# Agent attention with a maxout layer: one engine for each output tile of the last group, and new orders of work in the last batch

## The chip, the cores and the metric

The kernel runs on one core of a Trainium2 chip. The metric is the device time of one execution in microseconds; the runs shown of the kernel before have a median of 450.71 us (450.23 to 452.75, six runs). The profile comes from one execution, and its times count from the start of that execution's span.

## The reference

Four batches of 12544 queries, keys and values with 128 channels, and 49 agents per batch. First the agents attend to the keys and gather the values; then each query attends to the 49 agents; then a layer with three weight matrices takes the largest of three products and multiplies it with an output matrix:

```python
a2k = sm(agents, k)            # softmax(agents k^T / sqrt(128)), 49 x 12544 per batch
agent_v = a2k @ v              # 49 x 128 per batch
x = sm(q, agents) @ agent_v    # 12544 x 128 per batch
h = max(max(x @ w1, x @ w2), x @ w3)   # 50176 x 768
out = h @ w_out                # 50176 x 128
```

## The kernel before

Since x is a product with the small matrix agent_v, the kernel multiplies the weights with agent_v once per batch (the tile G, 49 rows at two heights, with columns for w2-w1, w3-w1 and the linear part through w1) and never forms x. It takes max(w1,w2,w3) as w1 plus the larger of (w2-w1) and the positive part of (w3-w1); the part w1 goes through the output matrix as a linear term.

The queries come in 49 groups (0 to 48) of 1024; 12 groups belong to a batch, and group 48 holds two row tiles of 128 of each of the four batches, so it has four parts (`parts_of`, L610). `q_group` (L617) names the steps of a group. For engine PE they are:

- scores `s` (L661) into a small PSUM tile, read by the exponentials `ex` on ACT (L669), and row sums `sum` (L673), read by the reciprocal `rec` on DVE (L680);
- for each of six column blocks f: `u`f (L694) and `v`f (L705), two matmuls each (eight in group 48). `a`f on ACT makes the positive part of u; `x`f on DVE takes the larger of v and a (L713) into the tile r. For f = 4 both `a4` and `x4` are on ACT, in place and then by L711;
- for each of the two output tiles o: `lin`o (L715, L718) starts the sum with two matmuls, and `oc`of (L722, L727) adds block f with four. `sc`o on DVE (L730, L734) scales it by the reciprocals into o_sb, and `st` (L739) stores a group with one DMA from SP.

In the text "38.x3" is step x3 of group 38. PSUM is short: all u and v tiles share three slots (`uv_tile`, L239), and scores, sums and output tiles share two (`small_tile`, L242). A step that opens a tile waits until the former holder of its slot has been read. The a tiles have three buffers, each r tile two, o_sb ten.

Keys and values of the next batch are worked through beside the queries (`k_group`, L509): group s of the queries carries a step of nine row tiles of keys, with `kc`, `vc`, `ea` on POOL (casts and the addition L547 to Eacc), `ks` and `kv` on PE, `ke` on ACT, `ka` on DVE. At a batch's end `k_tail` (L565) forms the new G: `red` (DVE, L574, over Eacc), `tot` (PE), `nrm` (DVE), products `p21` and `p31` (PE, L506), and their copies `e21` (DVE) and `e31a`, `e31b` (ACT). For the last batch this falls into groups 34 and 35.

The order is written by hand, as numbers: each step is filed under 6.0 times its group plus its place in a table, the list is sorted and emitted, and each engine runs its own instructions in that order. `places` (L808) chooses the table: KEY for most groups, LATE for groups 36 to 48, BORDER about a batch's end, OWN for single groups (34, 35, 36, 37, 47 and 48 among them), BATCH3 for the last `k_tail`. Stores are held back by up to seven groups (L824). Loads of q, their casts on POOL (`qc`) and, from group 36 on, transposes by DMA from SP (`turn_by_dma`, L657) run about two groups ahead.

Group 48 ends otherwise. Each of its two output tiles is scaled in halves, one per part, into four tiles o_end: half 2o by `end_scale` on DVE (L747, L749), half 2o+1 by `end_scale_scalar` on ACT (L752, L755, two instructions of 128 columns). Four stores of 128 KB (`end_store`, L757, L760) go from SP for parts 0 and 2 and from ACT for parts 1 and 3.

Of the kernel before, what the change touches and what calls it, by code (L numbers as in the profile page):

```python
# [25 lines left out]
    "oc14": 12.887, "oc12": 12.963, "oc13": 12.963, "sc1": 12.964, "st": 14.464,  # L26
}
LATE = {
    "s": -3.04749, "ex": -2.9048, "u1": -0.81512, "a1": -0.11576, "u2": 2.37421, "a2": 2.45765,
    "v1": 3.37564, "u3": 3.7004, "x1": 3.89334, "v2": 4.55864, "u0": 4.63, "a3": 4.65519, "x2": 4.7366,  # L30
    "a0": 5.00849, "v0": 5.38379, "u4": 5.77286, "x0": 6.25719, "a4": 6.54196, "u5": 7.04507,
    "v3": 7.1227, "x3": 7.44794, "v4": 7.51529, "lin1": 7.79655, "oc10": 8.14238, "sum": 8.14596,
    "rec": 8.17689, "oc12": 8.20379, "a5": 8.30536, "x4": 8.30648, "v5": 8.33752, "x5": 9.15285,
    "oc11": 9.49257, "oc13": 9.51825, "oc14": 10.09493, "lin0": 10.79959, "oc05": 10.84292,
    "oc15": 10.98413, "sc1": 11.49114, "oc02": 11.78965, "oc04": 11.82151, "oc00": 11.92155,
    "oc01": 12.02239, "oc03": 12.08397, "sc0": 12.87981, "st": 20.85007,
}

HEAD = {
# [27 lines left out]
        "st": 19.70003,  # L67
    },
    34: {
        "qt": -3.25348, "qe": -1.60938, "s": -1.08319, "ex": -0.07959, "ks": 0.24487, "ke": 0.69785,  # L70
        "u0": 0.71333, "a0": 1.42845, "v0": 1.46674, "u2": 1.55402, "ea": 1.95293, "u3": 2.01249,
        "sum": 2.04733, "kv": 2.10268, "a2": 2.26187, "a3": 2.44259, "u1": 3.00016, "x0": 3.08612,
        "v3": 3.16826, "rec": 3.3107, "ka": 3.48647, "a1": 4.24948, "x3": 4.28591, "v2": 4.7809,
        "u4": 4.96093, "x2": 5.54815, "a4": 6.34821, "u5": 6.35018, "a5": 6.53733, "v1": 6.53854,
        "v4": 6.56719, "x1": 6.7338, "x4": 6.84009, "v5": 6.91391, "x5": 6.9451, "lin1": 7.77018,
        "oc10": 8.3659, "lin0": 9.00035, "oc15": 9.04244, "oc04": 9.84141, "oc03": 10.06875,
        "oc01": 10.63146, "oc11": 10.91162, "oc00": 11.48787, "oc02": 11.69743, "oc05": 11.81297,
        "oc13": 11.92399, "sc0": 13.04207, "oc14": 13.24301, "oc12": 13.83351, "sc1": 15.27025,
        "st": 24.04256,
    },  # L80
    35: {
        "qt": -3.42697, "qe": -1.92735, "s": -1.33281, "ex": -1.31359, "ks": -0.92787, "sum": -0.87491,
        "ke": -0.36902, "kv": 0.32675, "ka": 0.59937, "rec": 0.88212, "u0": 0.88898, "a0": 0.90891,
        "v0": 1.17271, "u2": 1.45782, "a2": 2.00605, "u3": 2.51453, "x0": 2.59991, "v2": 2.93949,
        "a3": 3.20012, "u1": 3.23502, "a1": 3.44584, "x2": 3.51835, "v3": 3.942, "x3": 4.00627,
        "u5": 4.00643, "a5": 4.27302, "v5": 5.21895, "u4": 5.42122, "x5": 5.50884, "v1": 6.24909,
        "a4": 7.18659, "lin0": 7.89365, "oc03": 8.01405, "v4": 8.43263, "x1": 8.57785, "x4": 9.00519,
        "oc01": 9.40322, "oc02": 9.47513, "oc04": 10.01557, "oc00": 10.50745, "oc05": 10.70916,
        "lin1": 10.90156, "sc0": 11.20709, "oc15": 11.40347, "oc14": 11.51719, "oc11": 11.60961,
        "oc13": 13.16199, "oc12": 13.4014, "oc10": 13.57708, "sc1": 14.10054, "st": 28.07888,  # L90
    },
    36: {
        "s": -3.85762, "ex": -3.02118, "u1": -1.08192, "a1": 0.13487, "u2": 1.12084, "a2": 1.36634,
        "v2": 2.58017, "u0": 2.89822, "a0": 3.64302, "x2": 3.64864, "v1": 3.74492, "u3": 4.3491,
        "a3": 4.61245, "x1": 4.81452, "v0": 5.22302, "u4": 5.36733, "x0": 5.40904, "sum": 5.69395,
        "rec": 5.70943, "a4": 6.01497, "v3": 6.05388, "u5": 6.27145, "x3": 6.33451, "v4": 7.23655,
        "a5": 7.57697, "v5": 7.74872, "x4": 7.83644, "lin1": 7.8482, "oc10": 7.92453, "x5": 8.25933,
        "oc12": 8.53805, "oc14": 9.4705, "lin0": 10.11318, "oc00": 10.32008, "oc05": 11.08993,
        "oc11": 11.69579, "oc15": 11.95855, "oc13": 12.2097, "oc02": 12.27498, "sc1": 12.67367,
        "oc01": 13.63741, "oc04": 13.76201, "oc03": 14.31012, "sc0": 14.45082, "st": 20.04155,  # L100
    },
    37: {
        "s": -2.3763, "ex": -1.99168, "u1": -0.89023, "a1": -0.83864, "u2": 1.83631, "a2": 2.10039,
        "v2": 2.62074, "v1": 3.10251, "u0": 3.16911, "x2": 4.82079, "a0": 4.82575, "v0": 5.46426,
        "x1": 5.54152, "u3": 5.79276, "x0": 5.85326, "u5": 6.28625, "a3": 6.54158, "v3": 6.87889,
        "x3": 7.02476, "a5": 7.06215, "u4": 7.13124, "sum": 7.13155, "rec": 7.40011, "a4": 7.42192,
        "v5": 8.40138, "lin1": 8.44301, "x5": 8.50546, "oc11": 8.7139, "oc13": 8.85734, "v4": 9.11956,
        "oc10": 9.83416, "oc15": 9.91897, "lin0": 10.00468, "oc12": 10.1672, "x4": 10.46283,
        "oc02": 10.75773, "oc14": 10.97159, "oc01": 10.99548, "sc1": 11.08374, "oc05": 12.19635,
        "oc04": 12.41887, "oc00": 12.48727, "oc03": 12.57446, "sc0": 13.3308, "st": 13.63859,  # L110
    },
    47: {
        "s": -2.96572, "ex": -2.44054, "u1": -0.98286, "a1": -0.38292, "u0": 2.50098, "v1": 2.50777,
        "a0": 2.51445, "x1": 3.57249, "u2": 3.78871, "v0": 3.86021, "x0": 4.17982, "a2": 4.99948,
        "u3": 5.49603, "a3": 5.52978, "v2": 5.6013, "u4": 5.76145, "x2": 5.78978, "a4": 5.84387,
        "u5": 6.40472, "v4": 7.61729, "a5": 7.97742, "sum": 8.24781, "lin0": 8.29329, "oc00": 8.61937,
        "v3": 9.06308, "rec": 9.56376, "oc01": 10.03933, "x4": 10.07603, "x3": 10.6289, "v5": 10.86536,
        "lin1": 11.57727, "oc04": 11.9012, "oc14": 12.54349, "oc13": 13.40548, "x5": 13.64988,
        "oc02": 13.88884, "oc05": 14.16102, "oc03": 14.92264, "sc0": 16.27611, "oc12": 16.99023,
        "oc15": 17.06872, "oc11": 17.18888, "oc10": 17.27128, "sc1": 18.85812, "st": 23.913,  # L120
    },
    48: {
        "s": -3.4204, "ex": -2.49073, "u1": -1.6217, "a1": -0.87085, "v1": 0.78092, "x1": 2.62133,
        "u2": 4.49381, "a2": 4.991, "u0": 6.76262, "v2": 7.39248, "x2": 7.92987, "a0": 8.92021,
        "u5": 9.17989, "v0": 9.29415, "u4": 9.83418, "a5": 10.99894, "sum": 11.11918, "x0": 11.13319,
        "u3": 11.61847, "rec": 12.01294, "a4": 12.28323, "v5": 12.58725, "a3": 13.4554,
        "lin1": 13.86262, "oc10": 14.04021, "x5": 14.15402, "oc11": 14.85848, "v4": 16.25715,
        "x4": 17.85448, "v3": 19.03702, "lin0": 19.66535, "oc15": 20.01931, "oc01": 20.4512,
        "oc12": 22.46167, "x3": 24.03035, "oc05": 24.815, "oc14": 25.87451, "oc13": 26.8641,
        "sc1": 29.0489, "oc04": 29.05912, "oc03": 29.88451, "oc02": 30.80374, "sr1": 30.84707,  # L130
        "st2": 30.91835, "oc00": 43.00949, "st3": 43.44114, "sr0": 44.15505, "sc0": 47.77127,
        "st1": 53.21418, "st0": 99.95534,
    },
}
BORDER = {
# [48 lines left out]
    "e31b": 1.11618, "e21": 1.96962,  # L184
}
BATCH3 = {
    "red": -1.28697, "tot": 0.35013, "nrm": 0.77195, "p31": 0.91882, "e31a": 1.03104, "e31b": 1.44272,
    "p21": 2.07801, "e21": 2.88209,
}


# [1 line left out]
def kernel(  # L193
# [18 lines left out]
    nc = tc.nc  # L212
# [34 lines left out]
    def at(key, fn):  # L247
        ops.append((key, len(ops), fn))
# [368 lines left out]
    def q_group(s):  # L617
# [3 lines left out]
        key = 6.0 * s  # L621
        K = places(s)
# [124 lines left out]
        def end_scale(i):  # L747
            t, src = end_tile(i)
            nc.vector.tensor_tensor(out=t, in0=src, op=ALU.mult,  # L749
                                    in1=d["r"][:, 2 * i:2 * i + 2].unsqueeze(2).to_broadcast([P, 2, C]))  # L750
# [6 lines left out]
        def end_store(i):  # L757
            b, t0, j0, _ = parts[i]
            row = (b * NT + t0) * P
            (nc.scalar if i % 2 else nc.sync).dma_start(  # L760
                out[row:row + 2 * P, :].rearrange("(p j) c -> p j c", j=2), d["end", i])


# [14 lines left out]
        for o in range(2):  # L778
            at(key + K[f"lin{o}"], lambda o=o: out_linear(o))
            for f in range(NF):  # L780
                at(key + K[f"oc{o}{f}"], lambda o=o, f=f: out_hidden(o, f))
            if s < NQ - 1:
                at(key + K[f"sc{o}"], lambda o=o: out_scale(o))
            else:
                at(key + K[f"sc{o}"], lambda o=o: end_scale(2 * o))
                at(key + K[f"sr{o}"], lambda o=o: end_scale_scalar(2 * o + 1))
        if s < NQ - 1:
            at(key + K["st"], store)
        else:
# [96 lines left out]
```

## Time and profile before

| What | us |
|---|---|
| median of six runs | 450.71 |
| the profiled execution | 450.23 |
| its span, first to last instruction | 448.4 |
| PE, DVE, ACT busy in the span | 431.2, 403.3, 399.4 |
| group 33's u5 to the last output step of group 37 | 42.44 |
| from there to the last output step of group 45 (eight groups) | 61.69 |
| from there to the end of the span | 24.16 |

A line of the timeline or of a group gives engine, source line and operation, what is written and read, the count behind an x and, in brackets, the idle time before it with what ended it. A matmul line's time goes from the start of the first to the modelled end of the last. SPq and ACTq are the issue of DMAs. In a regular group the orders on the engines are these (a stroke marks a step of the next group, two strokes of the one after):

```
PE   u5 v3 v4 lin1 oc10 sum oc12 v5 u2' s'' v1' oc11 oc13 u3' oc14 v2' u0' lin0 oc05 oc15 u1'' v0' u4' oc02 oc04 oc00 oc01 oc03
ACT  a4 a5 x4 a2' ex'' a3' a0' a1''
DVE  sc0(of the group before) x3 rec x5 x1' x2' sc1 x0' sc0
```

### The profile page before, as it was taken

What the parts mean: (1) busy time and instruction counts of PE and PEld (TensorE: products, weight loads), DVE (VectorE), ACT (ScalarE), POOL (GpSimd) and SP (SyncE); (2) the same over time, 40 slices, a digit from 0 to 9 for tenths busy, and PEclk for the clock granted to TensorE, in tenths of its full rate; (3) what the DMA queues carried; (4) which work ended last, traced back from release to release, by engine and by line L of the source; (5) the groups of instructions that cost most, each with busy time, mean ns of one, the idle gap of its engine ahead of it and who ended that gap; (6) DMA issues with size and microseconds to landing.
All of it is one profiled execution on the core that took longest, in us unless ns stands there. A gap on an engine that the chain in (4) does not pass through costs nothing.

```text
span 448.4 us, 13332 instructions
## 1 busy us (share of the span) xinstructions
PE 431.2 (96%) x5506; PEld 276.8 (62%) x5506; DVE 403.3 (90%) x506; ACT 399.4 (89%) x463; POOL 169.2 (38%) x164
## 2 busy tenths in 40 slices
PE   3898999999999999999999999999999999999995
PEld 2665566666665666666665766666655555565665
DVE  2334999999999999999999999999999999999995
ACT  1557999999988999999989999999989999999994
POOL 4432465665332554554423445565310111111000
PEclk9999999999999999999999999999999999999999
DMA  8999999999569999999899999999878676566922
GB/s 315 415 411 367 278 265 276 288 321 265 157 204 351 298 312 294 306 317 280 261 278 270 286 319 274 299 330 295 230 220 182 173 213 153 156 188 177 387 96 96
DMA packets 83800, 118.87 MB, mean 265 GB/s; under 512 B 57687, under 2 KB 59803, under 8 KB 83739
## 3 DMA queue, kind: packets, MB, share of 16 engines
q1 hardware_dynamic: 83248, 117.66, 87.4%
q8 instruction: 43, 0.70, 0.6%
q10 hardware_dynamic: 491, 0.36, 0.2%
q14 instruction: 18, 0.15, 0.1%
HBM read 78.74 MB, written 25.69 MB: 233 GB/s over the span
## 4 chain that ended last, share of the span: by engine, by line
PE 84%; DMA 8%; DVE 3%; ACT 2%; issue 1%; ACTq 0%; SPq 0%; DVEq 0%
PE uv_ps L688 34%; PE o_ps L727 32%; PE o_ps L718 6%; DMA st<-in_v_dram 5%; PE m_ps L665 3%; PE m_ps L651 3%; DVE r L713 2%; DMA st<-in_moe_w_dram 2%; PE m_ps L535 2%; PE m_ps L366 2%; ACT a_sb L703 1%; PE m_ps L676 1%; DMA ag_st<-in_agents_dram 1%; PE uv_ps L506 1%; DVE o_sb L734 0%
## 5 line engine op out<-in xcount | busy, mean ns | idle before, releaser
L713 DVE TENSOR_TENSOR r<-uv_ps,a_sb 128x1024 bf16<-128x1024 f32 x245 | 297.5, 1222 | 9.7 <-PE uv_ps L688 5.5
L703 ACT ACTIVATE a_sb<-uv_ps 128x1024 bf16<-128x1024 f32 x245 | 243.5, 1024 | 16.7 <-PE uv_ps L688 12.6
L688 PE MATMUL uv_ps<-e_q,G 49*128 49x512 bf16 (+1 forms) x1248 | 181.6, 369 | 1.6 <-ACT G L433 0.5
L727 PE MATMUL o_ps<-wo_bf,r 128*128 128x128 bf16 x2352 | 176.3, 220 | 0.0
L727 PEld LDWEIGHTS <-r 128*128 128x128 bf16 x2352 | 139.7, 98 | 42.0 <-issue 39.2
L688 PEld LDWEIGHTS <-G 49*128 49x128 bf16 x1248 | 57.0, 93 | 62.1 <-issue 23.0
L646 POOL CAST q_bf<-st 128x1024 bf16<-128x1024 f32 x49 | 51.1, 1042 | 90.0 <-DMA st<-in_q_dram 79.2
L734 DVE TENSOR_TENSOR o_sb<-o_ps,recips 128x512 f32<-128x512 f32 x96 | 65.7, 685 | 2.4 <-PE o_ps L727 0.8
L515 POOL CAST k_bf<-st 128x1152 bf16<-128x1152 f32 (+1 forms) x33 | 37.5, 1136 | 62.8 <-DMA st<-in_k_dram 62.8
L519 POOL CAST v_bf<-st 128x1152 bf16<-128x1152 f32 (+1 forms) x33 | 37.6, 1140 | 47.5 <-DMA st<-in_v_dram 44.1
L711 ACT ACTIVATE r<-uv_ps 128x1024 bf16<-128x1024 f32 x49 | 50.2, 1025 | 1.9 <-PE uv_ps L688 1.6
L700 ACT ACTIVATE uv_ps<-uv_ps 128x1024 f32<-128x1024 f32 x49 | 49.6, 1012 | 0.0
L718 PE MATMUL o_ps<-G,e_q 128*128 128x256 bf16 x196 | 37.9, 275 | 0.0
L547 POOL TENSOR_TENSOR Eacc<-Eacc,e_k 128x441 f32<-128x441 f32 x27 | 27.7, 1025 | 22.1 <-ACT e_k L371 22.1
L671 ACT ACTIVATE e_q<-m_ps 128x512 bf16<-128x512 f32 x49 | 29.2, 596 | 1.7 <-PE m_ps L665 0.8
L380 DVE COPY kT<-uv_ps 128x1152 bf16<-128x1152 bf16 (+1 forms) x11 | 8.3, 752 | 18.0 <-PE uv_ps L377 18.0
L718 PEld LDWEIGHTS <-e_q 128*128 128x128 bf16 x196 | 11.8, 97 | 20.0 <-issue 19.5
L655 DVE COPY qT<-m_ps 128x1024 bf16<-128x1024 bf16 x34 | 23.3, 686 | 0.4 <-PE m_ps L651 0.4
L651 PE MATMUL m_ps<-ident,q_bf 128*128 128x128 bf16 x272 | 21.3, 222 | 0.0
L665 PE MATMUL m_ps<-qT,agT 128*64 128x512 bf16 (+1 forms) x104 | 20.1, 393 | 0.0
L371 ACT ACTIVATE e_k<-m_ps 128x441 bf16<-128x441 f32 (+1 forms) x33 | 17.8, 538 | 2.1 <-PE m_ps L676 0.7
L390 POOL CAST k_bf<-st 128x1152 bf16<-128x1152 f32 (+1 forms) x11 | 12.5, 1139 | 15.6 <-DMA st<-in_k_dram 15.6
(74 smaller groups left out, 224.6 us busy)
## 6 DMA issues: line engine op xcount, KB each, us to landing
st<-in_q_dram SPq DMA_DIRECT2D x48, 512.0 KB, 5.0
out_dram<-o_sb SPq DMA_DIRECT2D x48, 512.0 KB, 5.8
st<-in_k_dram SPq DMA_DIRECT2D x40, 576.0 KB, 5.0
st<-in_v_dram SPq DMA_DIRECT2D x40, 576.0 KB, 8.7
st<-in_k_dram SPq DMA_DIRECT2D x4, 512.0 KB, 6.9
st<-in_v_dram SPq DMA_DIRECT2D x4, 512.0 KB, 7.1
st<-in_moe_w_dram SPq DMA_DIRECT2D x2, 384.0 KB, 8.2
kT<-k_bf SPq DMA_TRANSPOSE x33, 4.2
```

Of the source, the lines that this page charges most:

```text
L515: nc.gpsimd.tensor_copy(out=d["kb"][:, :n, :], in_=d["k"][:, :n, :])
L519: nc.gpsimd.tensor_copy(out=d["vb"][:, :n, :], in_=d["v"][:, :n, :])
L646: nc.gpsimd.tensor_copy(out=d["qb"], in_=d["q"])
L651: nc.tensor.transpose(t[:, j * P:(j + 1) * P], d["qb"][:, j, :], ident)
L688: nc.tensor.matmul(t[:, h, j0 * P:j1 * P], G[b][h * H:h * H + A, col + f * P:col + (f + 1) * P], d["e"][h * H:h * H + A, j0 * P:j1 * P], s ...
L700: nc.scalar.activation(u, u, AF.Relu)
L703: nc.scalar.activation(a_sb[f], u, AF.Relu)
L711: nc.scalar.activation(r, v_ps[f], AF.Relu)
L713: nc.vector.tensor_tensor(out=r, in0=v_ps[f], in1=a_sb[f], op=ALU.max)
L718: nc.tensor.matmul(t[:, i * 2 * C:(i + 1) * 2 * C], d["e"][:, jj * P:(jj + 1) * P], G[batch[jj]][:, C1O:C1O + 2 * C], start=(i == 0), stop ...
L727: nc.tensor.matmul(t[:, c:c + C], r_sb[f][:, h, jj * P:(jj + 1) * P], wo_bf[:, f, :], start=False, stop=True, skip_group_check=True)
L734: nc.vector.tensor_tensor(out=d["out"][:, j:j + m, :], in0=d["o", o].rearrange("p (j c) -> p j c", c=C), in1=d["r"][:, j:j + m].unsqueeze( ...
```

## The change

In group 48, output tile 0 is scaled by DVE alone (two instructions) and tile 1 by ACT alone (four). Parts 0, 1 and 2 are stored from SP and part 3 from ACT. All numbers of LATE, of OWN for groups 34, 35, 36, 37, 47 and 48, and of BATCH3 are replaced. No instruction is added or removed.

In a regular group of the last batch PE's order becomes:

```
PE   sum u5 v3 v4 lin1 oc10 oc11 v5 u2' s'' v1' oc12 oc14 v2' u3' lin0 oc13 u0' oc15 oc00 oc03 u1'' v0' u4' oc01 oc05 oc02 oc04
```

ACT's and DVE's stay as they are there. At the border the product p21 comes ahead of p31 (it was the other way round), and most steps of groups 34 to 37 stand in another order. On POOL the cast of q of group 36 goes ahead of the last addition to Eacc. On SP the store of group 35 goes ahead of the load of q of group 41 (it stood behind the last transpose), and the stores of groups 34 and 36 go behind the last transpose. Group 48 ends on PE with

```
before   lin0 oc15 oc01 oc12 oc05 oc14 oc13 oc04 oc03 oc02 oc00
after    v5 oc12 oc14 oc13 lin0 oc01 oc00 oc04 oc15 oc03 oc02 oc05
```

```diff
 LATE = {
-    "s": -3.04749, "ex": -2.9048, "u1": -0.81512, "a1": -0.11576, "u2": 2.37421, "a2": 2.45765,
-    "v1": 3.37564, "u3": 3.7004, "x1": 3.89334, "v2": 4.55864, "u0": 4.63, "a3": 4.65519, "x2": 4.7366,
...
+    "s": -2.9742, "ex": -2.69831, "u1": -0.20723, "a1": 0.3452, "u2": 2.54405, "a2": 2.67071,
+    "v1": 3.40424, "v2": 3.6765, "x1": 3.90517, "u3": 3.96031, "x2": 4.37926, "a3": 4.48427,
...
     35: {
...
+        "st": -18.35646, "qt": -3.35196, "qe": -1.18286, "s": -0.90942, "ex": -0.27045, "u2": -0.10419,
...
 BATCH3 = {
-    "red": -1.28697, "tot": 0.35013, "nrm": 0.77195, "p31": 0.91882, "e31a": 1.03104, "e31b": 1.44272,
-    "p21": 2.07801, "e21": 2.88209,
+    "red": 0.66814, "tot": 1.38766, "nrm": 4.44362, "p21": 4.87002, "e21": 6.06012, "p31": 6.44574,
+    "e31a": 6.82772, "e31b": 7.06431,
 }
...
         def end_store(i):
             b, t0, j0, _ = parts[i]
             row = (b * NT + t0) * P
-            (nc.scalar if i % 2 else nc.sync).dma_start(
+            (nc.scalar if i == 3 else nc.sync).dma_start(
                 out[row:row + 2 * P, :].rearrange("(p j) c -> p j c", j=2), d["end", i])
...
-                at(key + K[f"sc{o}"], lambda o=o: end_scale(2 * o))
-                at(key + K[f"sr{o}"], lambda o=o: end_scale_scalar(2 * o + 1))
+                at(key + K[f"sc{o}"], lambda o=o: (end_scale_scalar if o else end_scale)(2 * o))
+                at(key + K[f"sr{o}"], lambda o=o: (end_scale_scalar if o else end_scale)(2 * o + 1))
```

## The prediction

> **What bounds the kernel now.** First the page's busy times, the chain that ended last and the costliest groups:
>
> ```profile
> PE 431.2 (96%) x5506; PEld 276.8 (62%) x5506; DVE 403.3 (90%) x506; ACT 399.4 (89%) x463; POOL 169.2 (38%) x164
> ...
> PE 84%; DMA 8%; DVE 3%; ACT 2%; issue 1%; ACTq 0%; SPq 0%; DVEq 0%
> ...
> L713 DVE TENSOR_TENSOR r<-uv_ps,a_sb 128x1024 bf16<-128x1024 f32 x245 | 297.5, 1222 | 9.7 <-PE uv_ps L688 5.5
> L703 ACT ACTIVATE a_sb<-uv_ps 128x1024 bf16<-128x1024 f32 x245 | 243.5, 1024 | 16.7 <-PE uv_ps L688 12.6
> L727 PE MATMUL o_ps<-wo_bf,r 128*128 128x128 bf16 x2352 | 176.3, 220 | 0.0
> ```
>
> PE heads the chain, DVE and ACT follow within 7%. So the next view is the busy time by stage, with borders where the new order begins (the fifth u of group 33, 320.15), where the regular groups begin and end (last step of groups 37 and 45), and the end:
>
> ```profile
> 320.15:362.59 42.44, 42.30 (x486) 25.15 (x484) 39.56 (x48) 39.00 (x46) 8.13 (x9) 1.00 0.78 199
> 362.59:424.28 61.69, 61.65 (x659) 35.90 (x657) 58.50 (x65) 59.59 (x65) 7.97 (x8) 1.00 0.71 205
> 424.28:448.44 24.16, 19.60 (x309) 14.32 (x306) 18.54 (x23) 17.14 (x21) 0.00 (x0) 1.00 0.29 112
> ```
>
> Columns: span, then PE, PEld, DVE, ACT, POOL, granted clock, DMA share, GB/s. The clock is full and DMA has room, so order alone matters. PE is "busy" throughout, but a matmul that waits to enter is hidden in that, so I read starts, in one regular group:
>
> ```profile
> 382.50 0.76 PE L688 MATMUL uv_ps<-e_q,G 49*128 49x512 bf16 x4
> ...
> 383.97 0.92 PE L688 MATMUL uv_ps<-e_q,G 49*128 49x512 bf16 x6
> ...
> 384.82 1.29 PE L727 MATMUL o_ps<-wo_bf,r 128*128 128x128 bf16 x20
> ...
> 386.05 0.82 PE L688 MATMUL uv_ps<-e_q,G 49*128 49x512 bf16 x6
> 386.15 0.69 DVE L734 TENSOR_TENSOR o_sb<-o_ps,recips 128x512 f32<-128x512 f32 x1
> ...
> 386.76 1.21 DVE L713 TENSOR_TENSOR r<-uv_ps,a_sb 128x1024 bf16<-128x1024 f32 x1
> ...
> 387.67 0.74 PE L688 MATMUL uv_ps<-e_q,G 49*128 49x512 bf16 x4
> ```
>
> A u or v step (two matmuls) costs PE 0.22 us after another, an oc step (four) 0.22 after another; between the two kinds it is 0.32 (20 matmuls from 384.82, next u at 386.05: 4 x 0.22 + 0.32). Three steps without a wait show 0.82, two 0.61. So 383.97 hides a wait of 0.10 (v0 for x2's tile), 382.50 one of 0.15 (u0 for x1), 387.67 one of 0.13 (u2 for x3, which ends at 387.97; u2 starts 388.03). The rest of PE's 7.71 per group is step after step.
>
> **The change, regular groups (38 to 45).** ACT's and DVE's orders stay. PE has the same 28 steps and 12 changes of kind; sum goes ahead of u5, v2 ahead of u3, lin0 ahead of u0. Walk, from the start of the group's last oc step:
> - Before: that step ends 0.39 later, sc0 at 0.42, x3 0.61 after it at 1.03, 1.21 long, u2 at 2.30. From u2 to the next last step 5.41 (5.16 of steps, 0.15 and 0.10 of waits). Sum 7.71.
> - After: sum at 0.22, u5 0.17 later, v3 at 0.61; its result (0.39, and 0.11 until DVE starts) lets x3 begin at 1.11; u2 at 2.39. Then 5.10 of steps: v2 now comes 0.6 before DVE wants it, so x2 follows x1 at 1.14 instead of 1.40 and v0's wait is gone; u0 falls at 4.98, just behind x1's end (4.93). New is 0.06 for u4, whose tile a0 frees at 6.56, as a3 starts 0.35 later than now (u3 behind v2). Sum 7.55.
>
> The gain is 0.16 x 8 = **1.3 us**. ACT's sequence then is a5 0.84, x4 1.76, a2 2.83, ex 3.75, a3 4.57, a0 5.49, a1 6.51, a4 7.43, next a5 8.39: it fits. So does lin1, which now needs the slot that sc0 frees (1.17) and is due at 1.15. Bounds: 0 if u0 still waits for x1 and lin1 for sc0, 0.25 per group if only the waits go: 0 to 2.0.
>
> **Border (groups 34 to 37).** Now, from PE's starts: 153 steps sum to 40.4 us at these prices (transposes, scores and products at their own), waits to 2.05 (33.v5 to 34.u0 0.21, 35.v4 to 36.v2 0.19, 36.v3 to 36.u5 0.17, 39.u1 to 38.v0 0.25, smaller ones), in all 42.44. After: the same steps, 55 changes of kind for 57, make 40.2. I walked them as above, each start the latest of PE's previous step, the freed tile and the operand, with 1.14 start to start for DVE maxima, 0.92 for ACT, 0.62 for scalings. Waits that remain: 34.u5 for x3 0.30, 36.v2 for 35.x1 0.24, 35.u1 for x2 0.22, 37.v5 for x0 0.15, 34.u3 0.14, 37.v1 0.10, smaller ones 0.5: 1.65. Sum 41.9, **gain 0.56**. Its tightest joint is new: the product for columns of w2-w1 (p21) now goes first and p31 needs the tile e21 frees; p31 is due at 337.18 and e21 ends 337.14. POOL now casts q of 36 (seen at 325.75) before the last Eacc addition, so that ends 327.8; behind it waits DVE's reduction, due 330.1: 2.3 us of cover. On SP the store of 35 goes ahead of q's load 41: its data is ready at 350, SP comes there at 357.6, so no wait; its issue (0.43) and 512 KB (1.7 us at 300 GB/s) push transpose 41 (363.3, landing 4.2) to about 369.6, and the scores want it at about 372. Cover 2.4 us; beyond it each us costs one. The stores of 34 and 36 move behind the last transpose, whose cover is the ten o_sb slots: the scalings of 46 and 47 need stores 38 and 39, issued after 413.7, at 429 and later. All this costs nothing. Bounds: -0.3 (all margins lost at e21) to 2.2 (no waits).
>
> **Tail.** Now:
>
> ```profile
> 443.11 0.43 DVE L749 TENSOR_TENSOR o_end<-o_ps,recips 128x256 f32<-128x256 f32 x1 [0.56 <-PE o_ps L727]
> 443.56 2.53 SPq L760 DMA_DIRECT2D out_dram<-o_end  x2
> 443.57 0.63 ACT L755 ACTIVATE o_end<-o_ps,recips 128x128 f32<-128x128 f32 x2 [1.17 <-DVE o_end L749]
> 444.23 0.38 ACTq L760 DMA_DIRECT2D out_dram<-o_end  x1
> 444.66 0.63 ACT L755 ACTIVATE o_end<-o_ps,recips 128x128 f32<-128x128 f32 x2 [0.46 <-ACT o_end L755]
> 445.31 0.34 ACTq L760 DMA_DIRECT2D out_dram<-o_end  x1
> 445.31 0.42 DVE L749 TENSOR_TENSOR o_end<-o_ps,recips 128x256 f32<-128x256 f32 x1 [1.78 <-ACT o_end L755]
> ```
>
> The halves of one tile run one after the other, ACT then DVE, with ACT's issue (0.38) between: last matmul ends 443.97, last scaling 445.73, end 448.44 (2.7 for issue, landing 1.7, finish). Walking groups 46 to 48 from group 45's last oc step: the last max (48.x5) ends at 18.8 (now 18.3), oc15 follows, then oc03, oc02, oc05, ending at 19.92 (now 19.69; 25 changes of kind for 23). Tile 1 is ACT's from 19.30 to 20.48; tile 0 is DVE's, two of 0.43, to 20.77. Store 0 follows store 1 on SP and leaves at 20.82; plus 2.7 the end is at 23.47, now 24.16: **gain 0.69**.
>
> Two rules of the Trainium skill speak against this. "ScalarE: Activation LUTs", Rules for kernel authors, sends multiplications to VectorE and budgets about 0.3 us plus 0.83 ns per element for an ACTIVATE. The row has 0.63 for two of 128, four 1.2; by the rule 1.6, ACT's store leaves at 21.0 and the gain falls to 0.5. I take the row. "DMA: Bandwidth & Descriptors", Issuing engines are not separate DMA queues, says that queues save only issue time and all transfers share 16 engines. Three stores of 128 KB now leave within 0.4 us; at that page's 436 GB/s each is 0.3 us, so by it store 0 could land 0.6 later, gain 0.1. The two last ones of now, 0.47 apart, still land in 1.7, so I take no delay. Bounds 0 to 0.9.
>
> **Sum.** 0.56 + 1.3 + 0.69 = 2.5 us. The profiled execution took 450.23, 448.4 of it span, 1.8 around. After: span 445.9, execution 447.7. The median of the runs shown is 0.5 above that execution: **448.2**.
>
> **Rivals.**
> - *The regular group stays at 7.71*, because u0 has only 0.05 us of margin behind x1 and lin1 none behind sc0; a slightly longer handover puts the waits back. For it: both are handovers I know only from neighbours. Against: x2 no longer waits. Border and tail remain: 450.7 - 1.25 = 449.5.
> - *The border loses nearly all its waits*, since late handovers early in the walk push everything behind them into cover: 2.2 for 0.56, time 446.6. Against: the e21 and x1 joints are arithmetic of busy rows.
> - *Slower*: lin1 is tied to sc0, and sc0 to x0. If x0 is late by d, sc0, lin1, x3 and u2 are all late by d, in each of 8 groups. Each 0.1 us costs 0.8. It decides from 0.33 per group above today's 7.71 (8.04: 2.6, against the 1.25 of border and tail): 452.1 or more. For it: sc0 could start at 0.37 and must at 0.43, so the margin is 0.06. Against: DVE's own sequence sums to 7.2.
>
> **How the numbers follow.** 0.3% (1.35 us) is about what a measurement tells from no change. Main case 0.64 (own range 447.0 to 449.3), waits back 0.17, waits gone 0.12, slower 0.07. Faster is the first and third, 0.76; same 0.17; slower 0.07. The range reaches to both neighbours, 446.6 to 450.0; above it lie the slower case and part of the second.
>
> **What would show it.** Right: 7.55 us from a group's last oc step to the next; the wait between v2 and u0 gone; x2 1.14 behind x1; DVE's last two scalings back to back after the last matmul and the end about 3.5 us behind it. Wrong: L665 waiting for a DMA near 373 us, DVE's reduction waiting for POOL, lin1 starting behind sc0 by over 0.1, or the last store landing in over 2 us.

## The result, and the profile after

The changed kernel takes 448.45 us (median of 32 runs, 448.06 to 451.03); in the same comparison the kernel before took 450.59 (69 runs). The ratio is 0.9952, 95% interval 0.9942 to 0.9961: about 2.1 us, or 0.5%, faster. 448.2 was forecast, with a range of 446.6 to 450.0.

The page of the changed kernel (behind the tables its lines are numbered one higher than before, as the table of group 47 has a line more):

```profile
PE 430.4 (96%) x5506; PEld 277.9 (62%) x5506; DVE 402.3 (90%) x506; ACT 397.3 (89%) x463; POOL 169.1 (38%) x164
...
PE 84%; DMA 8%; DVE 4%; ACT 1%; issue 1%; DVEq 0%; SPq 0%; ACTq 0%
...
L714 DVE TENSOR_TENSOR r<-uv_ps,a_sb 128x1024 bf16<-128x1024 f32 x245 | 296.8, 1222 | 11.0 <-PE uv_ps L689 7.2
L704 ACT ACTIVATE a_sb<-uv_ps 128x1024 bf16<-128x1024 f32 x245 | 242.8, 1024 | 17.4 <-PE uv_ps L689 15.5
L728 PE MATMUL o_ps<-wo_bf,r 128*128 128x128 bf16 x2352 | 175.1, 220 | 0.0
```

Counts and mean durations are those of before: only places have moved. The page's totals do not show the gain (this execution spent 449.55 us, span 447.8, and was in the head of the program 1.6 behind the other one, as the last section tells). The stages do. Their borders are the same instructions as before: u5 of group 33, the last output step of group 37, that of group 45, the end of the span. The columns are span, then PE, PEld, DVE, ACT, POOL, granted clock, DMA share and GB/s:

```profile
321.78:363.61 41.83, 41.69 (x487) 25.02 (x485) 39.38 (x48) 38.65 (x46) 7.09 (x8) 1.00 0.75 209
363.61:424.10 60.49, 60.36 (x659) 36.59 (x657) 57.46 (x65) 57.78 (x66) 8.12 (x8) 1.00 0.68 205
424.10:447.76 23.66, 19.66 (x309) 14.59 (x306) 18.68 (x23) 17.05 (x22) 0.00 (x0) 0.97 0.28 108
```

| Stage | before | forecast | after | gain forecast | gain measured |
|---|---|---|---|---|---|
| border (groups 34 to 37) | 42.44 | 41.9 | 41.83 | 0.56 | 0.61 |
| regular (38 to 45) | 61.69 | 60.4 | 60.49 | 1.3 | 1.20 |
| tail | 24.16 | 23.47 | 23.66 | 0.69 | 0.50 |
| sum | 128.29 | 125.8 | 125.98 | 2.5 | 2.31 |

PE in a regular group of the changed kernel (group 41 with the first steps of 42 and 43):

```profile
386.88 0.96 PE L689 MATMUL uv_ps<-e_q,G 49*128 49x512 bf16 x6
...
388.54 0.66 PE L689 MATMUL uv_ps<-e_q,G 49*128 49x512 bf16 x4
...
390.34 0.61 PE L689 MATMUL uv_ps<-e_q,G 49*128 49x512 bf16 x4
390.88 0.39 PE L719 MATMUL o_ps<-G,e_q 128*128 128x256 bf16 x2
391.11 0.39 PE L728 MATMUL o_ps<-wo_bf,r 128*128 128x128 bf16 x4
391.45 0.39 PE L689 MATMUL uv_ps<-e_q,G 49*128 49x512 bf16 x2
```

By the prices of before, three u or v steps in a row take 0.82 and two 0.61. So v2 and u3 (390.34) run without a wait, u5, v3 and v4 (386.88) hide 0.14 (v4 adds into the tile of u4, in which a4 works in place, and waits for a4), v5 and the next u2 (388.54) hide 0.05, and u0 (391.45) comes 0.34 behind the step before it, where a change of kind alone costs 0.32. The wait of v0 (0.10), nearly all of u0's (0.15) and most of u2's (0.13) are gone; v4's is new. That is the 0.18 between 7.71 and 7.53.

The tail of the changed kernel:

```profile
443.20 1.14 ACT L756 ACTIVATE o_end<-o_ps,recips 128x128 f32<-128x128 f32 x4 [1.75 <-PE o_ps L728]
443.85 1.31 SPq L761 DMA_DIRECT2D out_dram<-o_end  x3
443.87 0.76 DVE L750 TENSOR_TENSOR o_end<-o_ps,recips 128x256 f32<-128x256 f32 x2 [1.16 <-PE o_ps L728]
444.37 0.38 ACTq L761 DMA_DIRECT2D out_dram<-o_end  x1
```

ACT's four and DVE's two now overlap. The last matmul ends at 443.83 and the last scaling at 444.62, 0.8 behind it where it was 1.8, but the end comes 3.15 after that scaling where it was 2.70.

### The profile page after: what moved, and what is told of

Its sections match the earlier page's. It is cut to its first block, busy times and chain, and to the rows that moved or that the text cites. A ratio compares the mean times of both kernels' runs of the same rounds, so it can differ in the third digit from the quotient of the medians.

```text
span 447.8 us, 13331 instructions
## 1 busy us (share of the span) xinstructions
PE 430.4 (96%) x5506; PEld 277.9 (62%) x5506; DVE 402.3 (90%) x506; ACT 397.3 (89%) x463; POOL 169.1 (38%) x164
## 4 chain that ended last, share of the span: by engine, by line
PE 84%; DMA 8%; DVE 4%; ACT 1%; issue 1%; DVEq 0%; SPq 0%; ACTq 0%
PE uv_ps L689 34%; PE o_ps L728 31%; PE o_ps L719 6%; DMA st<-in_v_dram 5%; PE m_ps L652 3%; PE m_ps L666 3%; DVE r L714 3%; DMA st<-in_moe_w_dram 2%; PE m_ps L536 2%; PE m_ps L367 2%; PE m_ps L677 1%; DMA ag_st<-in_agents_dram 1%; ACT a_sb L704 1%; PE uv_ps L507 1%; DVE o_sb L735 1%
## 5 line engine op out<-in xcount | busy, mean ns | idle before, releaser
L516 POOL CAST k_bf<-st 128x1152 bf16<-128x1152 f32 (+1 forms) x33 | 37.5, 1136 | 64.3 <-DMA st<-in_k_dram 64.3
L652 PEld LDWEIGHTS <-q_bf 128*128 128x128 bf16 x272 | 16.8, 100 | 3.2 <-issue 2.8
```

Of the source, the lines that this page charges most:

```text
L516: nc.gpsimd.tensor_copy(out=d["kb"][:, :n, :], in_=d["k"][:, :n, :])
L652: nc.tensor.transpose(t[:, j * P:(j + 1) * P], d["qb"][:, j, :], ident)
```

## The experiments

All times are medians. Each kernel was measured beside the kernel before (450.59 beside the change, 450.74 to 450.81 beside the others). The stages come from one profiled execution of each kernel; where intervals are wide, they tell more. Here are the kernels with other orders, in us (those with another end have a table further on):

| Kernel | border | regular | tail | sum against before | median against before |
|---|---|---|---|---|---|
| before | 42.44 | 61.69 | 24.16 | | |
| the change | 41.83 | 60.49 | 23.66 | -2.3 | -2.1 |
| the change, again | 41.82 | 60.50 | 23.70 | -2.3 | -2.1 |
| LATE alone | 43.78 | 61.30 | 25.38 | +2.2 | +2.1 |
| border alone | 43.47 | 63.05 | 24.11 | +2.3 | +2.3 |
| end alone | 42.45 | 61.70 | 23.93 | -0.2 | -0.4 |
| border and LATE | 42.38 | 61.57 | 25.38 | +1.0 | +1.2 |
| LATE and end | 43.77 | 60.21 | 23.67 | -0.6 | -0.6 |
| v2 moved alone | 43.33 | 61.76 | 24.17 | +1.0 | +1.0 |
| v2 moved from group 39 on | 42.45 | 61.60 | 24.15 | -0.1 | +0.1 |

The sums of the three stages and the medians agree within about 0.2 us, so nothing outside these stages matters by more than that.

### One part at a time

The prediction added three gains as if each stood for itself. If so, each part alone must bring its own. Each of the first three kernels is the kernel before with one set of new numbers.

LATE alone:

```diff
 LATE = {
-    "s": -3.04749, "ex": -2.9048, "u1": -0.81512, "a1": -0.11576, "u2": 2.37421, "a2": 2.45765,
...
+    "s": -2.9742, "ex": -2.69831, "u1": -0.20723, "a1": 0.3452, "u2": 2.54405, "a2": 2.67071,
...
```

> Before, with only the new table LATE (groups 38 to 46). My theory, that the regular group falls from 7.71 to 7.55 us: eight groups give 1.2 to 1.3, time about 449.4, and from the last output step of group 37 to that of group 45 about 60.5 us in place of 61.69. Rival, that the gain sits in border and tail and the regular stage is shorter only because it is handed over differently: no change, 450.6.

Measured: 452.95, ratio 1.0043 (1.0029 to 1.0056), slower by 2.1 us. Its windows:

```profile
320.25:364.03 43.78, 42.84 (x487) 25.26 (x485) 39.76 (x48) 38.83 (x46) 9.30 (x9) 1.00 0.75 202
364.03:425.33 61.30, 60.40 (x660) 36.70 (x658) 56.87 (x65) 57.81 (x65) 8.32 (x8) 1.00 0.67 193
425.33:450.71 25.38, 19.90 (x309) 14.18 (x306) 19.06 (x23) 17.33 (x21) 0.00 (x0) 0.98 0.40 154
```

Both theories missed. Seven of the eight regular groups do take 7.53 (7.51 to 7.53), as forecast; the eighth takes 8.61, and border and tail are 1.3 and 1.2 longer. The loss sits where a group of the new table meets one of the old. The timeline at groups 46 and 47 (47 keeps its own old table) shows how:

```profile
422.82 0.60 PE L688 MATMUL uv_ps<-e_q,G 49*128 49x512 bf16 x4
423.25 1.94 ACT L703 ACTIVATE a_sb<-uv_ps 128x1024 bf16<-128x1024 f32 x2 [0.99 <-PE uv_ps L688]
424.32 0.39 PE L688 MATMUL uv_ps<-e_q,G 49*128 49x512 bf16 x2 [0.90 <-ACT a_sb L703]
...
425.22 1.22 DVE L713 TENSOR_TENSOR r<-uv_ps,a_sb 128x1024 bf16<-128x1024 f32 x1 [1.83 <-ACT a_sb L703]
```

The first line is 47.u1 and 46.v0. The old table of 47 puts 47.a1 ahead of 46.a0 on ACT, while the new numbers of 46 bring 47.u1 late on PE. ACT stands 0.99 for 47.u1 with 46.a0 behind it, though 46.u0 has been ready since about 422.1; PE's u4 then stands about 1.0 for the slot, and DVE 1.83 for 46.a0. In the border it is the same: 38.u1, now late, delays 38.a1, and behind it 37.a3 (354.77, before 353.80), whose slot 37.u4 needs: a wait of 0.70.

Border alone (groups 34 to 37 and BATCH3):

```diff
 BATCH3 = {
-    "red": -1.28697, "tot": 0.35013, "nrm": 0.77195, "p31": 0.91882, "e31a": 1.03104, "e31b": 1.44272,
-    "p21": 2.07801, "e21": 2.88209,
+    "red": 0.66814, "tot": 1.38766, "nrm": 4.44362, "p21": 4.87002, "e21": 6.06012, "p31": 6.44574,
+    "e31a": 6.82772, "e31b": 7.06431,
 }
...
     37: {
...
```

> Before, with only the new tables of groups 34 to 37 and of the last batch's tail of keys. My theory: the border's waits fall and two changes of kind go, 0.6 us less, time 450.0, stage about 41.8 in place of 42.44. Rival, that the new border needs the new LATE behind it (group 37's steps overlap with group 38's): the 0.6 is lost in groups 37 and 38, 450.6 or more.

Measured: 453.11, ratio 1.0050 (1.0032 to 1.0068), slower by 2.3: the rival's direction, at a price that it did not foresee. The parts of the border up to group 35 take their new length (20.73 and 7.71, as in the change); groups 36 and 37 lose, and group 38 takes 8.94. There:

```profile
367.62 0.39 PE L727 MATMUL o_ps<-wo_bf,r 128*128 128x128 bf16 x4
367.99 1.02 ACT L711 ACTIVATE r<-uv_ps 128x1024 bf16<-128x1024 f32 x1
368.43 0.68 DVE L734 TENSOR_TENSOR o_sb<-o_ps,recips 128x512 f32<-128x512 f32 x1
...
369.17 0.25 PE L676 MATMUL m_ps<-sel,e_q 128*128 128x2 bf16 x4 [1.16 <-DVE o_sb L734]
```

38.sum needs one of the two small tiles. Old LATE sends it right behind 38.oc10; new group 37 closes its second tile late, and 37.sc1 reads it until 369.11. The largest wait in groups 36 and 37 comes from another joint, on ACT: old LATE puts 38.ex (352.94) ahead of 36.x4 (353.44), where the change has 36.x4 first, and 37.u3, whose slot 36.x4 frees, waits 0.53.

End alone:

```diff
-            (nc.scalar if i % 2 else nc.sync).dma_start(
+            (nc.scalar if i == 3 else nc.sync).dma_start(
...
-                at(key + K[f"sc{o}"], lambda o=o: end_scale(2 * o))
+                at(key + K[f"sc{o}"], lambda o=o: (end_scale_scalar if o else end_scale)(2 * o))
...
     47: {
...
     48: {
...
```

> Before, with only the new tables of groups 47 and 48 and the new end (tile 1 scaled by ACT, tile 0 by DVE, three stores from SP). My theory: the end after the last matmul falls from 4.5 to about 3.9 us, with the last store landing some 0.45 later than before; 0.5 us gained, 450.1. Rival, that the tail's gain belongs to the order of the last groups as handed over by the new LATE: 450.6 or slower.

Measured: 450.41, ratio 0.9986 (0.9964 to 1.0007), not to be told from no change by the times. The tail is 0.23 shorter by the profile (23.93 for 24.16), half of what was expected: after the last matmul it ends at 3.94 for 4.47, but that matmul starts 0.31 later, since group 46 (7.84 for 7.62) meets the new 47.

### Two parts at a time

If the losses belong to the joints, they go when both sides of a joint are new, and stay where they are not. Two kernels test it; each is the change with one set of numbers put back.

The first, border and LATE, has this end again, with the former tables of groups 47 and 48:

```diff
-            (nc.scalar if i == 3 else nc.sync).dma_start(
+            (nc.scalar if i % 2 else nc.sync).dma_start(
...
-                at(key + K[f"sc{o}"], lambda o=o: (end_scale_scalar if o else end_scale)(2 * o))
+                at(key + K[f"sc{o}"], lambda o=o: end_scale(2 * o))
...
```

The second, LATE and end, has the former tables of groups 34 to 37 and of the tail of keys:

```diff
 BATCH3 = {
-    "red": 0.66814, "tot": 1.38766, "nrm": 4.44362, "p21": 4.87002, "e21": 6.06012, "p31": 6.44574,
-    "e31a": 6.82772, "e31b": 7.06431,
+    "red": -1.28697, "tot": 0.35013, "nrm": 0.77195, "p31": 0.91882, "e31a": 1.03104, "e31b": 1.44272,
+    "p21": 2.07801, "e21": 2.88209,
 }
```

> The change without its end: the new tables of groups 34 to 37 and LATE together, groups 47 and 48 as before. New theory from the runs of single parts: a table loses time only where it meets a table of the other set. Here the joint of groups 37 and 38 is whole and the joint of 46 and 47 broken: border 41.8 and seven groups of 7.53 as in the change, group 45 and the tail as with LATE alone (8.6 and 25.4), so 2.8 slower than the change: 451.2. Rival, that each part is slower by itself and adds up: 455.

> The change without its border: the new LATE and the new end with the tables of groups 47 and 48, groups 34 to 37 as before. By the same theory the joint of 46 and 47 is whole and that of 37 and 38 broken: border 43.8 as with LATE alone, then 60.3 and a tail of 23.7 as in the change: 1.9 slower than the change, 450.4. Rival, that each part adds up by itself: 452.5.

Measured: 451.98, ratio 1.0024 (1.0003 to 1.0046), and 450.11, ratio 0.9981 (0.9967 to 0.9994). The adding rival (455 and 452.5) is out. The windows of both, border and LATE first:

```profile
320.78:363.16 42.38, 41.89 (x486) 25.02 (x484) 39.92 (x48) 38.66 (x46) 8.21 (x8) 1.00 0.76 197
363.16:424.73 61.57, 60.54 (x659) 36.61 (x657) 56.84 (x65) 57.95 (x66) 8.32 (x8) 1.00 0.66 190
424.73:450.11 25.38, 19.90 (x310) 14.20 (x306) 19.07 (x23) 17.34 (x21) 0.00 (x0) 1.00 0.38 151
```

```profile
320.60:364.37 43.77, 42.84 (x486) 25.26 (x484) 39.74 (x48) 38.81 (x46) 8.98 (x9) 1.00 0.76 194
364.37:424.58 60.21, 60.21 (x659) 36.69 (x657) 57.47 (x65) 57.64 (x66) 7.29 (x7) 1.00 0.72 203
424.58:448.25 23.67, 19.66 (x309) 14.58 (x306) 18.68 (x23) 17.04 (x22) 0.00 (x0) 0.98 0.34 133
```

Where the end is old, group 45 takes 8.61 and the tail 25.38, to the hundredth as with LATE alone. Where the border is old, it takes 43.77 for 43.78 alone, and all behind it is as in the change, but for 0.3 us that the change loses in group 40 and this kernel does not (60.21 for 60.49; see the last section). The first kernel's border has 0.55 too much (42.38 for 41.83), whose cause is one instruction and is told in the last section; with it the 451.2 expected would be 451.8.

### One wait taken away

The walk said that a wait removed alone would come back at the next joint.

```diff
 LATE = {
-    "v1": 3.37564, "u3": 3.7004, "x1": 3.89334, "v2": 4.55864, "u0": 4.63, "a3": 4.65519, "x2": 4.7366,
+    "v1": 3.37564, "u3": 3.7004, "x1": 3.89334, "v2": 3.70, "u0": 4.63, "a3": 4.65519, "x2": 4.7366,
```

> Before, with one number of LATE changed: v2 moves ahead of u3 on PE, so that x2 can follow x1 and v0's wait of 0.10 per group should go. My theory, that a wait removed alone comes back at the next joint (u0 still waits for x1, and u4 then for a0): the regular group stays at 7.7, time 450.6 (450.4 to 450.8). Rival, that a wait seen is a wait to be gained: 0.10 to 0.25 in each of nine groups, 448.4 to 449.7.

Measured: 451.77, ratio 1.0027 (1.0015 to 1.0040), 1.0 slower. The regular groups take 7.70, as my theory had it: v0's 0.10 is gone, u4 waits 0.08 for a0, u0 still 0.16. But neither theory had the loss, which comes once, at group 38:

```profile
358.33 0.82 PE L688 MATMUL uv_ps<-e_q,G 49*128 49x512 bf16 x6
...
358.94 1.02 ACT L711 ACTIVATE r<-uv_ps 128x1024 bf16<-128x1024 f32 x1
...
360.01 0.39 PE L688 MATMUL uv_ps<-e_q,G 49*128 49x512 bf16 x2 [0.85 <-ACT r L711]
```

The first line is 37.v4, 38.v1 and 38.v2. There are three slots, and v2 and u3 take the next two that come free, in the order in which they stand. Now v2 takes 37.v5's and u3, which stood there before, is left with 37.v4's, which x4 on ACT reads until 359.96. If that is all, a swap that begins one group later must cost nothing. Beside the line above, this kernel gives group 38 the old numbers:

```diff
+    38: {
+        "v1": 3.37564, "u3": 3.7004, "x1": 3.89334, "v2": 4.55864, "u0": 4.63,
...
+    },
```

> As the swap of v2 ahead of u3, but group 38 keeps its former order, so that the swap begins at group 39. Theory: the 1.0 us that the swap lost sat at group 38 alone, where u3 took the slot of 37.v4, which 37.x4 reads late; here no step meets it, and the wait removed from v0 still comes back at the next joint: 450.7, no change to before, regular groups of 7.70. Rival, that the swap costs wherever it begins: 451.8.

Measured: 450.87, ratio 1.0012 (0.9993 to 1.0031): no change, with 7.70 in each regular group and 42.45 in the border. The rival (451.8) is out. Moving v2 alone gains 0.01 per group; the change's 0.18 takes the other moves with it, so that u0 and u2 too come just behind what they wait for.

### The end: who scales, and how stores land

Four kernels are the change with another end. The first has the old assignment of engines and stores under the new orders:

```diff
-            (nc.scalar if i == 3 else nc.sync).dma_start(
+            (nc.scalar if i % 2 else nc.sync).dma_start(
...
-                at(key + K[f"sc{o}"], lambda o=o: (end_scale_scalar if o else end_scale)(2 * o))
+                at(key + K[f"sc{o}"], lambda o=o: end_scale(2 * o))
...
```

> The changed kernel with the old assignment at the end: each output tile's halves scaled one by DVE and one by ACT, stores 1 and 3 from ACT, all orders as in the change. My theory, that the assignment and not the order shortens the end: the halves of a tile run one after the other again and the last scaling ends about 0.4 later, of which the landing gives back up to 0.3 as stores leave further apart: 0.1 to 0.4 slower than the changed kernel, 448.6 to 448.9. Rival, that the order of the last steps does it: no difference, 448.45.

Measured: 449.16, ratio 0.9968 (0.9951 to 0.9985), tail 24.44 for 23.66. The assignment brings 0.78 us of the tail, more than expected (by the medians, 1.6 below the kernel before where the change has 2.1, it is 0.5); the new order of the last steps by itself costs 0.28 (24.44 for 24.16 before). With the old assignment the last scaling ends 2.0 behind the last matmul instead of 0.8:

```profile
442.91 0.43 DVE L750 TENSOR_TENSOR o_end<-o_ps,recips 128x256 f32<-128x256 f32 x1 [0.49 <-PE o_ps L728]
...
443.37 0.63 ACT L756 ACTIVATE o_end<-o_ps,recips 128x128 f32<-128x128 f32 x2 [2.21 <-DVE o_end L750]
444.03 0.38 ACTq L761 DMA_DIRECT2D out_dram<-o_end  x1
444.46 0.63 ACT L756 ACTIVATE o_end<-o_ps,recips 128x128 f32<-128x128 f32 x2 [0.46 <-ACT o_end L756]
...
445.12 0.42 DVE L750 TENSOR_TENSOR o_end<-o_ps,recips 128x256 f32<-128x256 f32 x1 [1.78 <-ACT o_end L756]
```

Halves of one tile never run side by side here: DVE's last waits for ACT's. Then I asked why the last store lands late. One kernel leaves stores 2 and 3 out, one scales all four halves on DVE, one has that and stores 1 and 3 on ACT:

```diff
-            for i in range(4):
+            for i in range(2):
```

```diff
-                at(key + K[f"sc{o}"], lambda o=o: (end_scale_scalar if o else end_scale)(2 * o))
-                at(key + K[f"sr{o}"], lambda o=o: (end_scale_scalar if o else end_scale)(2 * o + 1))
+                at(key + K[f"sc{o}"], lambda o=o: end_scale(2 * o))
+                at(key + K[f"sr{o}"], lambda o=o: end_scale(2 * o + 1))
```

```diff
-            (nc.scalar if i == 3 else nc.sync).dma_start(
+            (nc.scalar if i % 2 else nc.sync).dma_start(
```

> The changed kernel without the stores of parts 2 and 3 of group 48 (it leaves out these rows of the output; their scalings are made). Theory that the last store lands late since three stores share the way: with two of the four stores, store 1 is alone behind store 0, and the end comes 2.7 us after the last scaling in place of 3.14: 0.45 less, 448.0. Rival, that the landing is long for another reason (the last issue on SP, or what closes the program): 3.1 us, no change, 448.45.

> The changed kernel with all four halves of group 48 scaled by DVE (four of about 0.38 us in place of two, ACT has none). Theory that the stores' crowding sets the last landing: tile 1's stores leave at about 443.7 and 444.1 and the last two 0.4 apart, the last landing falls by 0.3 to 0.4 and the last scaling comes no more than 0.1 later: 448.2. Rival, that the last scaling sets the end: DVE comes later to tile 0, 0.1 to 0.2 slower, 448.6.

> The changed kernel with all four halves of group 48 scaled by DVE and stores 1 and 3 issued by ACT, so that no store stands behind another's issue. Theory: the last store leaves 0.09 earlier than with three stores on SP and lands as late or earlier: end 3.3 after the start of the last matmul's step less 0.1, 447.7. Rival, that the issue is not what delays it: 447.8, as all four halves on DVE alone.

Measured: 448.36 (ratio 0.9944, 0.9922 to 0.9966), 447.80 (0.9931, 0.9903 to 0.9960) and 448.32 (0.9949, 0.9931 to 0.9967). The landing is the time from the start of the last store's issue to the end of SP's wait for it at the program's end:

| Kernel | stores' issues start, before the last one's | landing | tail |
|---|---|---|---|
| before | 2.20, 1.54, 0.46 | 1.72 | 24.16 |
| two stores alone | 0.42 | 1.80 | 23.51 |
| all four halves on DVE | 1.09, 0.76, 0.42 | 1.82 | 23.40 |
| the same, two queues | 1.00, 0.67, 0.19 | 2.00 | 23.49 |
| the change | 0.90, 0.43, 0.38 | 2.07 | 23.66 |

The closer together the stores leave, the later the last lands. The traces show why. In the change the core's 16 DMA engines are full while the data of the last three stores move; in the kernel before they stand empty ahead of the last two (the DMA share, the last number but one, is 1.02 and 0.00):

```profile
445.25:446.25 1.00, 0.00 (x0) 0.00 (x0) 0.00 (x0) 0.00 (x0) 0.00 (x0) 0.93 1.02 341
```

```profile
445.65:446.15 0.50, 0.00 (x0) 0.00 (x0) 0.09 (x1) 0.00 (x0) 0.00 (x0) 1.00 0.00 0
```

At 341 GB/s a store of 128 KB takes 0.38 us (an estimate from this row). If the four pass one after the other, the last waits 0.33 in the change, 0.19 with two queues, 0.05 with all halves on DVE and not at all with two stores; over the 1.72 of before they measured 0.35, 0.28, 0.10 and 0.08. So the stores share the way, and that is most of the delay; up to 0.09 is not explained by it. With two stores the last lands 0.27 sooner than with four, but only 0.15 of it reaches the end, as that kernel passes its closing waits 0.12 later. Its expectation (448.0) was too low, as was the idea that the sharing is worth the whole 0.45: 0.09 of that is store 0's issue standing behind store 1's on SP (scaled by 444.62, issued at 444.75), and 0.35 is the landing, of which taking two stores away returned 0.27.

All four halves on DVE spread the stores, and the last scaling comes no later:

```profile
441.90 1.43 DVE L750 TENSOR_TENSOR o_end<-o_ps,recips 128x256 f32<-128x256 f32 x4 [0.49 <-PE o_ps L728]
442.35 1.51 SPq L761 DMA_DIRECT2D out_dram<-o_end  x3
442.69 0.38 ACTq L761 DMA_DIRECT2D out_dram<-o_end  x1
```

That tail is 0.26 us shorter than the change's, and 447.80 is the lowest median of all; by the times alone (0.9903 to 0.9960 beside 0.9942 to 0.9961) it cannot be called faster than the change. Two stores from each queue did not help: the last issue came 0.19 behind another and landed in 2.00. That kernel's median is 0.5 above the one with all halves on DVE, and its tail explains only 0.09 of it; in its profiled execution the border took 0.71 longer, for a cause told in the last section. Its median is above both its theory (447.7) and its rival (447.8), which its interval doesn't exclude.

The change once more:

> The changed kernel once more, for a profile in which the clock is not reduced near 40 us: all stages as in its first profile, 33.u5 at 320.2 to 321, border 41.8, eight groups 60.5 with group 39 to 40 longer by 0.3, tail 23.7; time 448.4.

Measured: 448.63, ratio 0.9952 (0.9930 to 0.9975), with the stages as expected: 41.82, 60.50 and 23.70, each within 0.04 of the first profile's.

## Why the prediction was right

- **Border, 0.56 forecast, 0.61 measured.** Right, and the split fits as far as the traces tell it. With each start set against the plain cost of its pair of steps, the waits fall by 0.3 to 0.4, depending on what is taken as plain, where I had 0.40; the other 0.2 to 0.3 lies in the steps, where I had 0.2. The waits named are there (34.u5 0.24 for 0.30, 36.v2 0.25 for 0.24, 34.u3 0.14, 37.v1 0.14 for 0.10), but 35.u1 has 0.04 in place of 0.22, and 35.v0 has 0.10 that I did not name. p31 did not wait for e21, though with no margin (it starts at its plain distance of 0.32 and 0.07 behind e21's end), and no score waited for a transpose: in this execution none of the queue moves cost anything.
- **Regular groups, 7.55 forecast, 7.53 measured.** The walk held: x2 starts 1.13 behind x1 (1.14), v0's wait is gone, lin1 comes right behind v4. The wait that I put at u4 (0.06) sits at v4 (0.14) instead, and u2's fell by more than I had. That the total fits to 0.02 is in part luck: u2 comes 2.32 behind the last step (2.39 walked) and the rest takes 5.21 (5.16), two errors that cancel. Seven groups gain 0.18, 1.26 in all; group 40 takes 7.82 once, which brings the stage to 1.20.
- **Tail, 0.69 forecast, 0.50 measured: a size was off.** The mis-sized term is "plus 2.7", the time from the last scaling to the end. It measured 3.15, and one of the prediction's own signs of being wrong came true: the last store landed in over 2 us (2.07). The last scaling itself came 0.25 earlier than walked (20.52 behind group 45's last step, for 20.77), which gave half of it back. Of the two rules that I weighed there, ScalarE's did not come true (four ACTIVATEs took 1.14 us, as the row said, not 1.6). The one on the shared 16 engines ("DMA: Bandwidth & Descriptors", Issuing engines are not separate DMA queues) did, in about half its size: about 0.35 in landing where my estimate from that page's 436 GB/s gave 0.6 and I took 0. The engines moved 341 GB/s, but the earlier stores were partly through when the last left. The row I leaned on, two stores 0.47 apart, was the wrong neighbour for three in 0.43.
- **The sum** of the stages, 2.3, reached the median almost whole: 2.1.
- **The rivals.** Of the waits in the regular group only v4's 0.14 is new, they did not all go at the border, and sc0 never held lin1. But the mechanism of the slower rival, one late step that holds everything behind it, is what made LATE alone and the border alone slower; it stood at the joints between tables, and I had looked for it inside the regular group.
- **What the prediction did not see** is that its three gains are not three. It walked the change whole, so each joint was in its sums; to read them as gains of parts would have been wrong by over 6 us for LATE and border together (+2.1 and +2.3 alone, -1.9 by the sum).

## What to carry to other kernels

A hand-written order on engines that run in sequence is one piece: before testing or taking over a part of it, look at the first group on either side, where a tile slot or an in-order queue joins old and new. A wait in a trace is a gain only if the steps behind it can move up too; walk to the next joint first. At the end of a program, cost the last store by the others that leave within half a microsecond of it, not by a lone one.

## What the runs showed of the hardware that was not expected

**One small DVE instruction waits for POOL.** At the end of the last batch's keys the product k_recip x Vacc (L588, 128x49, both inputs in SBUF) stands ahead of p21 and p31. It takes 0.21 us in most profiles, but not where a cast of q has begun on POOL before it. The change again, and the kernel with all halves on DVE and two queues:

```profile
335.22 0.22 DVE L588 TENSOR_TENSOR avT<-Vacc,k_recip 128x49 bf16<-128x49 f32 x1
335.31 1.04 POOL L647 CAST q_bf<-st 128x1024 bf16<-128x1024 f32 x1 [5.55 <-PE uv_ps L689]
335.70 0.14 PEld L507 LDWEIGHTS <-avT 128*64 128x64 bf16 x4
```

```profile
334.61 1.04 POOL L647 CAST q_bf<-st 128x1024 bf16<-128x1024 f32 x1 [5.44 <-PE uv_ps L689]
334.80 0.92 DVE L588 TENSOR_TENSOR avT<-Vacc,k_recip 128x49 bf16<-128x49 f32 x1
335.77 0.14 PEld L507 LDWEIGHTS <-avT 128*64 128x64 bf16 x4 [0.60 <-DVE avT L588]
```

In the second it ends at 335.72, just behind the cast (335.65), and the border takes 42.53 for 41.82: the 0.71 that the instruction took longer. The same holds for border and LATE together (0.77, border 0.55 longer) and for two stores alone (0.34, border 0.12 longer). It was there to be read before the change: the same product at the end of an earlier batch stands behind a cast of k in all 14 profiles, takes 0.57 to 0.87 us and ends 0.06 to 0.07 behind the cast, in the kernel before too:

```profile
131.45 1.15 POOL L515 CAST k_bf<-st 128x1152 bf16<-128x1152 f32 x1 [5.83 <-DMA st<-in_k_dram]
132.03 0.64 DVE L587 TENSOR_TENSOR avT<-Vacc,k_recip 128x49 bf16<-128x49 f32 x1
```

The Trainium skill states it in "SBUF — State Buffer", Who interferes with whom: a DVE instruction with two SBUF inputs contends with a GpSimd instruction that reads SBUF, over ports that one of them locks, and the order of issue decides who is blocked. These traces agree for a product that comes second; a cast that came second (335.31 above) shows its usual 1.04, so the other direction is not shown here. Which comes first changes from execution to execution, as the cast waits for a load or a release; this joint is probably part of the scatter of the changed kernel, and the prediction did not look for it. A cast placed behind the product would settle it; that was not tried.

**A loss of 0.3 us that stays open.** In every profile with the new border the group that holds 40.x0 is longer than its neighbours (7.82 to 7.84 for 7.53; with the old LATE 7.83 for 7.71); with the old border it is not. In the changed kernel DVE starts that instruction at 378.30, though the wait ahead of it ended at 377.90 and nothing else is shown between. Why is not known.

**The clock in the head.** The first profile of the change had one stretch between 40 and 50 us, in code that the change does not touch, with a lower granted clock (0.50 from 44 to 46 us):

```profile
40.00:50.00 10.00, 8.78 (x71) 4.05 (x72) 6.91 (x12) 7.78 (x10) 4.85 (x5) 0.83 1.00 295
```

In the second profile the same stretch had 1.00. Group 1's u0 starts at 50.48 in the first and at 49.17 in the second, and u5 of group 33 at 321.78 and 320.64: that is the difference between 449.55 and 448.44 for the two executions. Comparing stages by their lengths, not by their times from the start, keeps such an event out.
